# Converting float64 weights beside attention: the integer words in PSUM, the raw words in eleven buffers, and four stages a slot apart

## The chip, the cores and the metric

The kernel runs on one core of a Trainium2 chip. The core has TensorE (PE in the profile; its weight loads are PEld), VectorE (DVE), ScalarE (ACT), GpSimd (POOL) and SyncE (SP, which here only issues DMA transfers). SBUF is the on-chip memory of 128 partitions, PSUM the memory into which TensorE writes its products. The metric is the device time of one execution in microseconds (us). Each engine works through a queue of its own in a fixed order; a queue stands still while its next instruction waits for another engine or a transfer.

## The reference

Two steps follow each other. The first is attention over q, k and v of 4 batches, 8 heads, 768 positions, 64 dimensions, where a query sees the 8 first keys of its sequence and the 96 keys up to itself, with a bias by distance that has its own slope for each head:

```
scores = q @ k.T / 8 - slope[h] * dist      (-1e9 where not kept)
a = softmax(scores);  x = a @ v             x: [4, 768, 512]
```

The second is a channel mix over x, with weights w_k [512, 1024], w_v [1024, 512], w_r [512, 512] that come as float64:

```
xk = mu_k * x + (1 - mu_k) * x_prev         x_prev: the position before
xr = mu_r * x + (1 - mu_r) * x_prev
k = relu(xk @ w_k);  r = sigmoid(xr @ w_r)
out = r * ((k * k) @ w_v)
```

## The kernel before

**Tiles and chunks.** The 3072 positions are 24 tiles of 128 queries, and two tiles make a chunk of 256 positions for the channel mix, so there are 12 chunks. A loop over steps takes one tile at a time, in four slots (the loop variable hp, two heads each). In a slot stand the transposes of the tile before, the scores of this tile and pieces of channel mix of an earlier chunk; at a step's start stand the products with v of the tile two before.

**Attention of a tile.** Scores are products into PSUM; for the first seven tiles (NATIVE) they are plain float32 products (L287, with queries and keys in qz and kz), from tile 7 on they are products of float32r parts (L289, L290). VectorE adds the bias and takes the row's extreme (L295), ScalarE takes exp with the row sum (L296), VectorE makes the reciprocal r (L302, L303), GpSimd multiplies e by r (L306), TensorE transposes e (L317), ScalarE copies the transposes out of PSUM (et, L318), TensorE multiplies with v (av, L334), ScalarE copies the result to x (L345). Tiles 0, 6, 12 and 18 start a sequence and have 128 keys in place of 256.

**Channel mix.** Every factor is split in two float32r parts, hi and lo, and each product is hi·hi + lo·hi + hi·lo (L371, L372, L373). mix makes xk and xr: the part of x_prev on ScalarE for chunk 0 and on GpSimd for the others (L355, L357), the sum on VectorE (L358), hi on ScalarE (L359), lo on VectorE (L360). Products kp with w_k follow; each of the four results per chunk becomes kk (relu L397, square L398, hi L399, lo L400). Then come products z with w_r, the sigmoid, products vps with w_v, the last product on VectorE (L414), and the store. Chunk 0's channel mix is put in the queue at step 3, and slots then take up to five pieces each.

**Weights.** A float64 weight is made into hi + lo in blocks of 128 rows and 512 columns: 8 blocks of w_k, 4 of w_r, 8 of w_v, 20 in all (L140). A block comes by one transfer of 512 KB as pairs of 32-bit words (L159). ScalarE takes the absolute value of the upper words with a scale (L166, L169). A second scaling follows: on GpSimd for blocks 0 to 7 (L167), while blocks 8 to 19 are bounded on VectorE by a max and a min (L170). Three integer operations on VectorE build the float32 words: shift and mask (L171), sign (L172), bits of the lower word (L173). All of this is in place, in an SBUF tile a. Then hi is a copy in float32r on ScalarE (L174) or GpSimd (L196, pool_copy), two blocks each in turn, and lo = a - hi is a subtraction on GpSimd (L180).

**Where the raw words lie.** Blocks of w_r and w_v take a buffer of the pool p4k (tag t4k, three buffers), which serves the queries and keys of later tiles and the temporary of mix as well. Blocks of w_k take buffers of the channel mix (kk_hi, kk_lo, xk_hi, xk_lo, xr_hi, xr_lo) ahead of chunk 0. btmp, in which the bias patterns are made, has the buffer kk_hi.

**What sets the order.** The program is written for the Tile framework, which gives out a pool's buffers and lays down one order per engine by a planner with a cost model of its own. The source sets the sequence of requests: at the end of each slot (slot = 4 * step + hp) weights_go begins blocks up to a pace and ends those up to one fewer:

```
n = min(8, 2 + slot * 4 // 3) if slot < 6 else 8 + (slot - 5) * 6 // 7
weights_go(n, n - 1 if n <= len(w_steps) else n)
```

channel_mix also calls weights_need ahead of products, which forces what is not yet requested.

Of the kernel before, what the change touches and what calls it, by code (L numbers as in the profile page):

```python
# [33 lines left out]
def tile_biased_attention_channel_mix(ctx: ExitStack, tc: tile.TileContext, qT, kT, v, n_sizes, mu_kr, w_k, w_v, w_r, q_rows, k_rows, v_rows, slopes, out):  # L34
# [55 lines left out]
    # The distance; n_local for a key that is only global, which is over any distance of a local key;  # L90
    # FAR or more where masked: such a key's weight is exactly 0.
# [13 lines left out]
    # 96 keys before the tile, then the tile's own  # L105
# [9 lines left out]
    # tile 0  # L115
# [11 lines left out]
    # later tiles: 32 keys from the start, 96 keys before the tile, the tile  # L127
# [15 lines left out]

    def weight_begin(i):
        # A float64 weight's words: (sign, 11 exponent bits, 20 bits), (32 bits).
        # a: its first 24 significant bits as a float32; hi: a rounded to float32r; lo: the rest of a.
        name, src, k, c = w_steps[i]
        if name != "k":
            raw = p4k.tile([128, 512, 2], I32, tag="t4k", name=f"w64_{i}")
            a = f2_pool.tile([128, 512], I32, tag="f2", name=f"wa_{i}")  # L150
        elif k < 2:
            both = f_pool.tile([128, 2048], I32, tag=("kk_hi", "kk_lo")[k], name=f"w64_{i}")
            raw = both[:, 0:1024].rearrange("p (n w) -> p n w", w=2)
            a = both[:, 1024:1536]
        else:
            t = "xk" if k == 2 else "xr"
            raw = f_pool.tile([128, 512, 2], I32, tag=t + "_hi", name=f"w64_{i}")
            a = f_pool.tile([128, 512], I32, tag=t + "_lo", name=f"wa_{i}")
        nc.sync.dma_start(raw.rearrange("p n w -> p (n w)"), src[k * 128 : (k + 1) * 128, 2 * c : 2 * c + 1024])  # L159
        low, top = raw[:, :, 0], raw[:, :, 1]  # L160
        hi = wts[name][0][:, k, c : c + 512]
        # top's bits as a float32: times 2**-112 (or 2**16, which differs in a bit that the shift drops) moves the float64
        # exponent's bias to the float32's. What float32 cannot hold is bounded: from 2**128 up (by Inf, which stays Inf,
        # or the min) to a large number, under 2**-127 (by underflow or the max) to 0.
        if i < 8:
            act.activation(a.bitcast(F32), top.bitcast(F32), AF.Abs, scale=2.0**111)  # L166
            pool.tensor_scalar(a.bitcast(F32), a.bitcast(F32), 2.0**-112, 2.0**-111, op0=ALU.mult, op1=ALU.mult)  # L167
        else:
            act.activation(a.bitcast(F32), top.bitcast(F32), AF.Abs, scale=2.0**16)  # L169
            vec.tensor_scalar(a.bitcast(F32), a.bitcast(F32), 2.0, HUGE, op0=ALU.max, op1=ALU.min)  # L170
        vec.tensor_scalar(a, a, 3, 0x7FFFFFF8, op0=ALU.logical_shift_left, op1=ALU.bitwise_and)  # L171
        vec.scalar_tensor_tensor(a, top, -0x80000000, a, op0=ALU.bitwise_and, op1=ALU.bitwise_or)  # L172
        vec.scalar_tensor_tensor(a, low, 29, a, op0=ALU.logical_shift_right, op1=ALU.bitwise_or)  # L173
        (act.copy if i % 4 < 2 else pool_copy)(hi, a.bitcast(F32))  # L174
        w_live[i] = a
# [6 lines left out]
    w_count = [0, 0]  # L182

    def weights_go(begun, ended):
        while w_count[0] < min(begun, len(w_steps)):
            weight_begin(w_count[0])
            w_count[0] += 1
        while w_count[1] < min(ended, w_count[0]):
            weight_end(w_count[1])
            w_count[1] += 1  # L190
# [8 lines left out]
    state = {}  # L199
    # the first tiles' queries and keys, with 64 rows of zeros: products of all 128 rows keep the tensor engine's clock up  # L200
# [223 lines left out]
    LAG = 3  # tiles from a chunk's first to the start of its channel mix  # L424
# [214 lines left out]
```

## Time and profile before

| | |
|---|---|
| median of 3 runs | 526.06 us (525.92 to 526.25) |
| profiled execution: first to last instruction (span) | 524.1 us |
| what lies around the span, median less span | 1.96 us |
| PE busy | 495.9 us (95%) |
| DVE busy | 372.4 us (71%) |
| ACT busy | 323.6 us (62%) |
| POOL busy | 283.0 us (54%) |
| DMA | 48.16 MB, mean 92 GB/s |

The profiled execution's own time is taken as its span with those 1.96 us around it. A row of the page's groups or of an answer on groups reads: line, engine, operation, output<-input, shape, count | busy us, mean ns of one | idle time of the engine just before it, and what ended it. A row of waits reads: engine and line that waited <- engine and line that ended the wait: us in total, times, longest. A row of the timeline begins with its start and its length in us.

### The profile page before, as it was taken

The numbers are of one execution on the slowest core, as the hardware profiler recorded it, in microseconds if no ns is written. First come the engines' busy times: TensorE is split into PE (matmuls) and PEld (weight loads), VectorE is DVE, ScalarE is ACT, GpSimd is POOL, SyncE is SP. The second block draws the span as 40 slices with busy tenths as digits, with TensorE's granted clock in tenths as the row PEclk, the third lists the DMA queues.
The fourth block names the chain that finished last, engine by engine and source line by source line (L and its number), as shares of the span: only waits on it lengthen the run. The fifth ranks groups of instructions, "written<-read, shape, count | busy, mean of one in ns | idle before, by whom it ended". The sixth has DMA issues, their size and how long they took to land.

```text
span 524.1 us, 9900 instructions
## 1 busy us (share of the span) xinstructions
PE 495.9 (95%) x3466; PEld 427.2 (82%) x3466; DVE 372.4 (71%) x854; ACT 323.6 (62%) x730; POOL 283.0 (54%) x410
## 2 busy tenths in 40 slices
PE   7885888979999999999999999999999999999995
PEld 4563766869898898898898898898898898898984
DVE  6799999987677766767767867767777865535321
ACT  4868585823957856846847757756757667643220
POOL 8799977987355644544547645535547634203000
PEclk9979799999999999999999999999999999999999
DMA  8998268150350530530521431521422210000101
GB/s 197 322 232 198 67 185 188 41 144 20 107 134 6 141 107 5 157 91 8 162 76 38 130 86 34 133 86 59 124 62 66 62 46 26 35 12 2 41 1 44
DMA packets 27304, 48.16 MB, mean 92 GB/s; under 512 B 7216, under 2 KB 13360, under 8 KB 27248
## 3 DMA queue, kind: packets, MB, share of 16 engines
q1 hardware_dynamic: 27104, 47.46, 34.0%
q8 instruction: 29, 0.48, 0.4%
q14 instruction: 27, 0.22, 0.1%
q10 hardware_dynamic: 144, 0.00, 0.0%
HBM read 41.16 MB, written 6.29 MB: 91 GB/s over the span
## 4 chain that ended last, share of the span: by engine, by line
PE 80%; DVE 11%; POOL 5%; issue 3%; DMA 1%; ACT 0%; DVEq 0%; POOLq 0%
PE vps L372 8%; PE vps L373 8%; PE vps L371 8%; PE kp L371 8%; PE kp L373 8%; PE kp L372 8%; PE av L334 7%; PE t L317 6%; PE z L371 4%; PE z L373 4%; PE z L372 4%; PE s L290 3%; PE s L289 3%; POOL e L306 2%; PE s L287 2%
## 5 line engine op out<-in xcount | busy, mean ns | idle before, releaser
L306 POOL TENSOR_SCALAR e<-e,r 128x256 f32<-128x256 f32 (+1 forms) x192 | 106.1, 570 | 137.0 <-DVE r L303 91.9
L371 PE MATMUL kp<-xk_hi,wk_hi 128*128 128x256 f32 x384 | 108.0, 282 | 0.2 <-DVE kk L398 0.2
L373 PE MATMUL kp<-xk_hi,wk_lo 128*128 128x256 f32 x384 | 107.5, 280 | 0.5 <-POOL wk_lo L180 0.5
L372 PE MATMUL kp<-xk_lo,wk_hi 128*128 128x256 f32 x384 | 107.3, 279 | 0.0
L296 ACT ACTIVATE e<-e,nmax 128x256 f32<-128x256 f32 (+1 forms) x192 | 92.6, 484 | 22.0 <-DVE nmax L295 21.0
L295 DVE CUSTOM_DVE_ANT_0 e<-s,pat 128x256 f32<-128x256 f32 (+1 forms) x192 | 69.0, 395 | 31.0 <-PE s L290 21.2
L372 PE MATMUL vps<-wv_lo,kk_hi 128*128 128x512 f32 x192 | 76.0, 396 | 2.6 <-POOL wv_lo L180 2.6
L371 PE MATMUL vps<-wv_hi,kk_hi 128*128 128x512 f32 x192 | 75.9, 395 | 0.4 <-POOL wv_hi L196 0.4
L373 PE MATMUL vps<-wv_hi,kk_lo 128*128 128x512 f32 x192 | 75.8, 395 | 0.0
L371 PEld LDWEIGHTS kp<-xk_hi,wk_hi 128*128 128x128 f32 x384 | 72.9, 190 | 1.2 <-DVE kk L398 0.6
L373 PEld LDWEIGHTS kp<-xk_hi,wk_lo 128*128 128x128 f32 x384 | 72.8, 190 | 0.9 <-POOL wk_lo L180 0.9
L372 PEld LDWEIGHTS kp<-xk_lo,wk_hi 128*128 128x128 f32 x384 | 72.9, 190 | 0.6
L318 ACT COPY et<-t 128x512 f32<-128x512 f32 (+1 forms) x96 | 52.0, 546 | 20.2 <-PE t L317 19.7
L317 PE MATMUL t<-ident,e 128*128 128x128 f32 x352 | 57.5, 280 | 5.7 <-POOL e L306 5.6
L398 DVE TENSOR_TENSOR kk<-kp,kk 128x512 f32<-128x512 f32 x48 | 33.1, 689 | 41.2 <-ACT kk L397 41.0
L317 PEld LDWEIGHTS t<-ident,e 128*128 128x128 f32 x352 | 41.2, 141 | 19.1 <-POOL e L306 9.2
L334 PE MATMUL av<-et,va 128*64 128x128 f32 x704 | 49.4, 284 | 0.6 <-ACT et L318 0.6
L334 PEld LDWEIGHTS av<-et,va 128*64 128x64 f32 x704 | 40.3, 139 | 10.5 <-issue 5.8
L400 DVE TENSOR_TENSOR kk_lo<-kk,kk_hi 128x512 fp32r<-128x512 f32 x48 | 35.3, 735 | 17.4 <-ACT kk_hi L399 17.3
L399 ACT CAST kk_hi<-kk 128x512 fp32r<-128x512 f32 x48 | 29.8, 622 | 25.6 <-DVE kk L398 25.6
L397 ACT ACTIVATE kk<-kp 128x512 f32<-128x512 f32 x48 | 28.3, 590 | 26.7 <-PE kp L373 24.5
L372 PEld LDWEIGHTS vps<-wv_lo,kk_hi 128*128 128x128 f32 x192 | 36.0, 187 | 10.5 <-POOL wv_lo L180 3.1
(103 smaller groups left out, 1051.1 us busy)
## 6 DMA issues: line engine op xcount, KB each, us to landing
kraw<-in_kT_dram SPq DMA_DIRECT2D x36, 256.0 KB, 3.9
qraw<-in_qT_dram SPq DMA_DIRECT2D x34, 256.0 KB, 4.1
va<-in_v_dram SPq DMA_DIRECT2D x24, 256.0 KB, 3.1
out_dram<-sig SPq DMA_DIRECT2D x24, 256.0 KB, 3.5
w<-in_w_k_dram SPq DMA_DIRECT2D x8, 512.0 KB, 9.1
w<-in_w_v_dram SPq DMA_DIRECT2D x8, 512.0 KB, 3.5
kz<-in_kT_dram SPq DMA_DIRECT2D x8, 256.0 KB, 6.7
w<-in_w_r_dram SPq DMA_DIRECT2D x4, 512.0 KB, 9.3
```

The lines of the kernel that those rows point to most:

```text
L295: vec.tensor_tensor_reduce(out=e[:, :w], in0=o, in1=p[:, h, :], op0=ALU.add, op1=ALU.min, scale=-0.125, scalar=3.0e38, accum_out=s["nmax"] ...
L296: act.activation(e[:, :w], e[:, :w], AF.Exp, bias=s["nmax"][:, h : h + 1], scale=-1.0, accum_out=s["sum"][:, h : h + 1])
L306: pool.tensor_scalar(e[:, :w], e[:, :w], r[:, u : u + 1], 1.0, op0=ALU.mult, op1=ALU.mult)
L317: pe.transpose(pt[:, c : c + 128], e[:, k * 128 : (k + 1) * 128], ident)
L318: act.copy(et[:, : 2 * nb * 128], pt[:, : 2 * nb * 128])
L334: pe.matmul(o, vt[:, h * 64 : (h + 1) * 64], et[:, c : c + 128], start=k == 0, stop=k == nb - 1)
L371: pe.matmul(o, sh, mh, start=first, stop=False)
L372: pe.matmul(o, sh, ml, start=False, stop=False)
L373: pe.matmul(o, sl, mh, start=False, stop=last)
L398: vec.tensor_mul(kk, pv, kk)
L399: act.copy(kkh[:, 2 * fp : 2 * fp + 2, :], kk)
L400: vec.tensor_sub(kkl[:, 2 * fp : 2 * fp + 2, :], kk, kkh[:, 2 * fp : 2 * fp + 2, :])
```

## The change

The weights' work is cut into four functions, which the loop requests at the start of each slot, each at a pace of its own.

- weight_load only takes a buffer and issues the transfer. Raw words lie in eleven buffers: blocks 0 to 2 and 11 to 19 in t4k, blocks 3 to 6 in xk_hi, xr_hi, xk_lo, xr_lo, blocks 7 and 8 in the two halves of kk_lo, blocks 9 and 10 in those of kk_hi.
- weight_begin takes a tile a from the pool f2 for every block, has ScalarE take the absolute value (L163) and GpSimd do the second scaling (L164), now for all 20 blocks. The max and min on VectorE are gone.
- weight_bits does the three integer operations (L174, L175, L176). The words between them lie in bits, a PSUM tile of the pool ps_f, whose three banks kp, z and vps use; the third operation writes back to a. The copy to hi follows.
- weight_end is as before (L182).

With w_pace(slot), a slot requests ends up to w_pace(slot - 2), integer work up to w_pace(slot - 1), begins up to w_pace(slot) and loads up to w_pace(slot) + 5. Two loads are requested ahead of the loop. Comments were taken out as well, so that lines have other numbers after the change: scores L288, L290 and L291, e L296, r L303 and L304, normalise L307, transposes L318, av L335, mix L359 (sum) and L361 (lo), products L372 to L374, hi copies on GpSimd L197, transfers of weights L155, of queries and keys L224 to L232.

```diff
     w_live = {}
 
+    w_raw, w_two = {}, []
+
+    def weight_load(i):
+        name, src, k, c = w_steps[i]
+        if i < 3 or i > 10:
+            raw = p4k.tile([128, 512, 2], I32, tag="t4k", name=f"w64_{i}")
+        elif i < 7:
+            raw = f_pool.tile([128, 512, 2], I32, tag=("xk_hi", "xr_hi", "xk_lo", "xr_lo")[i - 3], name=f"w64_{i}")
+        else:
+            if i % 2:
+                w_two.append(f_pool.tile([128, 2, 512, 2], I32, tag=("kk_lo", "kk_hi")[i // 2 - 3], name=f"w64_{i}"))
+            raw = w_two[-1][:, (i - 7) % 2]
+        nc.sync.dma_start(raw.rearrange("p n w -> p (n w)"), src[k * 128 : (k + 1) * 128, 2 * c : 2 * c + 1024])
+        w_raw[i] = raw
+
     def weight_begin(i):
...
+        a = f2_pool.tile([128, 512], I32, tag="f2", name=f"wa_{i}")
+        act.activation(a.bitcast(F32), w_raw[i][:, :, 1].bitcast(F32), AF.Abs, scale=2.0**111)
+        pool.tensor_scalar(a.bitcast(F32), a.bitcast(F32), 2.0**-112, 2.0**-111, op0=ALU.mult, op1=ALU.mult)
+        w_live[i] = a
+
+    def weight_bits(i):
...
-        if i < 8:
-            act.activation(a.bitcast(F32), top.bitcast(F32), AF.Abs, scale=2.0**111)
-            pool.tensor_scalar(a.bitcast(F32), a.bitcast(F32), 2.0**-112, 2.0**-111, op0=ALU.mult, op1=ALU.mult)
-        else:
-            act.activation(a.bitcast(F32), top.bitcast(F32), AF.Abs, scale=2.0**16)
-            vec.tensor_scalar(a.bitcast(F32), a.bitcast(F32), 2.0, HUGE, op0=ALU.max, op1=ALU.min)
-        vec.tensor_scalar(a, a, 3, 0x7FFFFFF8, op0=ALU.logical_shift_left, op1=ALU.bitwise_and)
-        vec.scalar_tensor_tensor(a, top, -0x80000000, a, op0=ALU.bitwise_and, op1=ALU.bitwise_or)
-        vec.scalar_tensor_tensor(a, low, 29, a, op0=ALU.logical_shift_right, op1=ALU.bitwise_or)
+        bits = ps_f.tile([128, 512], I32, name=f"wb_{i}", tag="f")
+        vec.tensor_scalar(bits, a, 3, 0x7FFFFFF8, op0=ALU.logical_shift_left, op1=ALU.bitwise_and)
+        vec.scalar_tensor_tensor(bits, top, -0x80000000, bits, op0=ALU.bitwise_and, op1=ALU.bitwise_or)
+        vec.scalar_tensor_tensor(a, low, 29, bits, op0=ALU.logical_shift_right, op1=ALU.bitwise_or)
         (act.copy if i % 4 < 2 else pool_copy)(hi, a.bitcast(F32))
...
+    def w_pace(slot):
+
+        return max(0, min(8, slot * 4 // 3 + 1) if slot < 6 else 8 + (slot - 5) * 5 // 4)
+
     load_tile(0)
     split_tile(0)
+    weights_go(0, 2)
...
         for hp in range(4):
+            slot = 4 * step + hp
+            weights_go(3, w_pace(slot - 2))
+            weights_go(2, w_pace(slot - 1))
+            weights_go(1, w_pace(slot))
+            weights_go(0, w_pace(slot) + 5)
...
-            slot = 4 * step + hp
-            n = min(8, 2 + slot * 4 // 3) if slot < 6 else 8 + (slot - 5) * 6 // 7
-            weights_go(n, n - 1 if n <= len(w_steps) else n)
```

The planner lays down another order for the first seven tiles. TensorE is shown first, where channel mix starts: s, t, av are scores, transposes and products with v; the number at a name's end is a tile's allocation. Before, the first kp stands among the transposes of tile 4, right behind the scores s_2 of that tile:

```order
96 L287 MATMUL s_2_890<-kz_178,qz_177 128x256 x2
97 L334 MATMUL av_729<-et_3_676,va_305 64x128
98 L334 MATMUL av_729<-et_3_676,va_413 64x128
99 L334 MATMUL av_729<-et_3_676,va_305 64x128
100 L334 MATMUL av_729<-et_3_676,va_413 64x128
101 L317 MATMUL t_0_750<-ident,e_0_582 128x128 x2
102 L371 MATMUL kp<-xk_hi,wk_hi 128x256 x2
103 L317 MATMUL t_0_750<-ident,e_1_585 128x128 x2
```

Now it stands behind the last scores of tile 6 (s_3_1441) and six of that tile's eight transposes:

```order
159 L288 MATMUL s_3_1441<-kz_178,qz_177 128x128 x2
160 L318 MATMUL t_1_1311<-ident,e_3_1118 128x128 x2
...
168 L318 MATMUL t_1_1561<-ident,e_3_1324 128x128
169 L318 MATMUL t_2_1610<-ident,e_4_1389 128x128
170 L318 MATMUL t_2_1610<-ident,e_5_1392 128x128
171 L372 MATMUL kp<-xk_hi,wk_hi 128x256 x2
172 L373 MATMUL kp<-xk_lo,wk_hi 128x256
173 L374 MATMUL kp<-xk_hi,wk_lo 128x256
```

What moved is chunk 0's channel mix, from tile 4's scores to behind tile 6's. Rows 171 to 467 now hold 192 kp, 42 z and 48 vps products and the products of tile 5 with v; at row 468 come tile 7's first scores. That row was row 467 before, and from there on both orders read alike.

On VectorE the place is the mix of chunk 0 (mix_k, and xk_lo which the first kp's last part needs). Before, it stands among blocks 5 to 7 and the scores of tiles 3 and 4:

```order
120 L171 TENSOR_SCALAR wa_322<-wa_322 128x512
121 L172 SCALAR_TENSOR_TENSOR wa_322<-w_6_321,wa_322 128x512
122 L358 SCALAR_TENSOR_TENSOR mix_k<-x_424,mus,mix_k 128x256
...
127 L358 SCALAR_TENSOR_TENSOR mix_k<-x_424,mus,mix_k 128x256
128 L173 SCALAR_TENSOR_TENSOR wa_322<-w_6_321,wa_322 128x512
129 L171 TENSOR_SCALAR w_5_291<-w_5_291 128x512
130 L358 SCALAR_TENSOR_TENSOR mix_k<-x_424,mus,mix_k 128x256 x2
```

Now it stands behind block 17 and among block 18, when the scores of all seven tiles have been taken:

```order
215 L304 RECIPROCAL r_3_1450<-r_3_1450 128x4
216 L174 TENSOR_SCALAR wb_707<-wa_673 128x512
217 L175 SCALAR_TENSOR_TENSOR wb_707<-w_17_494,wb_707 128x512
218 L176 SCALAR_TENSOR_TENSOR wa_673<-w_17_494,wb_707 128x512
219 L359 SCALAR_TENSOR_TENSOR mix_k<-x_461,mus,mix_k 128x256
220 L174 TENSOR_SCALAR wb_733<-wa_712 128x512
221 L359 SCALAR_TENSOR_TENSOR mix_k<-x_461,mus,mix_k 128x256 x2
```

The mix moved from block 6's integer work to that of blocks 17 and 18. The third place is SP's queue of transfers ahead of tile 2's queries and keys. Before:

```order
7 L239 DMA va_192<-in_v_dram 128x512
8 L159 DMA w_1_211<-in_w_k_dram 128x1024
9 L159 DMA w_2_238<-in_w_k_dram 128x1024
10 L159 DMA w_3_257<-in_w_k_dram 128x1024
11 L230 DMA kz_178<-in_kT_dram 64x8x32
12 L223 DMA qz_177<-in_qT_dram 64x1024
```

Now, with two weight blocks ahead of tile 1's data as well (rows 4 and 5):

```order
10 L155 DMA w_2_201<-in_w_k_dram 128x1024
11 L155 DMA w_3_203<-in_w_k_dram 128x1024
12 L155 DMA w_4_205<-in_w_k_dram 128x1024
13 L155 DMA w_5_207<-in_w_k_dram 128x1024
14 L155 DMA w_6_226<-in_w_k_dram 128x1024
15 L155 DMA w_7_255<-in_w_k_dram 128x1024
16 L155 DMA w_7_255<-in_w_r_dram 128x1024
17 L155 DMA w_9_279<-in_w_r_dram 128x1024
18 L224 DMA qz_177<-in_qT_dram 64x1024
```

Tile 2's queries moved from behind three weight blocks to behind ten.

More of the change, by code (lines that the diff above doesn't have):

```diff
@@ L29 @@
 FAR = 1.0e12
-HUGE = (1.875 - 2.0**-13) * 2.0**32
 @with_exitstack
@@ L142, in tile_biased_attention_channel_mix @@
     w_live = {}
-    def weight_begin(i):
-        name, src, k, c = w_steps[i]
[L148 to L154, printed above, removed]
-        else:
[L156 to L159, printed above, removed]
+    w_raw, w_two = {}, []
@@ L160, in weight_begin @@
+    def weight_begin(i):
+        a = f2_pool.tile([128, 512], I32, tag="f2", name=f"wa_{i}")
[3 more added lines that the diff above has]
+    def weight_bits(i):
+        name, src, k, c = w_steps[i]
+        a, raw = w_live[i], w_raw.pop(i)
         low, top = raw[:, :, 0], raw[:, :, 1]
         hi = wts[name][0][:, k, c : c + 512]
-        if i < 8:
-            act.activation(a.bitcast(F32), top.bitcast(F32), AF.Abs, scale=2.0**111)
-            pool.tensor_scalar(a.bitcast(F32), a.bitcast(F32), 2.0**-112, 2.0**-111, op0=ALU.mult, op1=ALU.mult)
-        else:
-            act.activation(a.bitcast(F32), top.bitcast(F32), AF.Abs, scale=2.0**16)
-            vec.tensor_scalar(a.bitcast(F32), a.bitcast(F32), 2.0, HUGE, op0=ALU.max, op1=ALU.min)
@@ L174, in weight_begin @@
+        vec.scalar_tensor_tensor(a, low, 29, bits, op0=ALU.logical_shift_right, op1=ALU.bitwise_or)
         (act.copy if i % 4 < 2 else pool_copy)(hi, a.bitcast(F32))
-        w_live[i] = a
     def weight_end(i):
@@ L180, in weight_end, with weights_go @@
         pool.tensor_sub(lo, w_live.pop(i).bitcast(F32), hi)
[L182 to L190, printed above, removed]
+    w_stages = (weight_load, weight_begin, weight_bits, weight_end)
+    w_count = [0, 0, 0, 0]
+    def weights_go(stage, n):
+        while w_count[stage] < min(n, len(w_steps)):
+            w_count[stage] += 1
+            w_stages[stage](w_count[stage] - 1)
     def weights_need(n):
-        weights_go(n, n)
+        for stage in range(4):
+            weights_go(stage, n)
     def pool_copy(dst, src):
```

## The prediction

> **What bounds the kernel now.** I read the page's busy times first, then windows by stage, then what TensorE waited for in the first 120 us, then the groups of VectorE and GpSimd there. In the windows the columns are PE, PEld, DVE, ACT and POOL busy time with counts, then the granted TensorE clock, the DMA share and GB/s.
>
> ```profile
> PE 495.9 (95%) x3466; PEld 427.2 (82%) x3466; DVE 372.4 (71%) x854; ACT 323.6 (62%) x730; POOL 283.0 (54%) x410
> ```
>
> ```profile
> 0.00:40.00 40.00, 32.13 (x150) 21.16 (x150) 32.23 (x116) 26.27 (x79) 34.45 (x52) 0.91 1.05 251
> 40.00:80.00 40.00, 30.91 (x212) 24.81 (x212) 38.69 (x89) 29.42 (x78) 34.77 (x40) 0.91 0.54 144
> 80.00:120.00 40.00, 34.40 (x229) 28.45 (x228) 37.24 (x70) 21.35 (x47) 33.06 (x35) 1.00 0.49 127
> 120.00:400.00 280.00, 280.00 (x2070) 249.07 (x2071) 205.59 (x457) 187.50 (x414) 148.85 (x227) 1.00 0.30 82
> 400.00:524.10 124.10, 118.49 (x814) 103.72 (x810) 58.62 (x126) 59.10 (x114) 31.93 (x59) 0.99 0.11 35
> ```
>
> From 120 to 400 us TensorE is busy without a gap. Of its 28.2 us of idle time (524.1 - 495.9), 22.6 lie before 120 us (7.9 + 9.1 + 5.6) and 5.6 in the tail. The page would call the kernel TensorE's, but a change to the weights can move only the first 120 us, and there VectorE and GpSimd are the full engines: between 40 and 80 us VectorE works 38.7 of 40 us. What TensorE waited for says the same:
>
> ```profile
> PE s L287 <- DVE nmax L295: 6.8, 3, 3.2
> PE t L317 <- POOL e L306: 5.6, 10, 1.2
> PE vps L372 <- POOL wv_lo L180: 2.6, 2, 1.8
> ```
>
> So the useful question is at which time TensorE reaches the stretch that it alone bounds, and how much of its work it has then done.
>
> **The mark.** The two TensorE orders shown with the change meet at the first score product of tile 7. Behind that row they read alike, and before it both hold the same products. Before, TensorE gets there at 131.63:
>
> ```profile
> 54.79 0.48 PE L371 MATMUL kp<-xk_hi,wk_hi 128*128 128x256 f32 x2
> 58.31 0.42 PE L371 MATMUL kp<-xk_hi,wk_hi 128*128 128x256 f32 x1
> 58.52 0.41 PE L372 MATMUL kp<-xk_lo,wk_hi 128*128 128x256 f32 x1
> 62.24 0.28 PE L372 MATMUL kp<-xk_lo,wk_hi 128*128 128x256 f32 x1
> 62.95 0.28 PE L372 MATMUL kp<-xk_lo,wk_hi 128*128 128x256 f32 x1
> 131.63 0.37 PE L289 MATMUL s<-kw,qh 128*128 128x256 f32 x1
> 133.60 0.39 PE L371 MATMUL vps<-wv_hi,kk_hi 128*128 128x512 f32 x1
> 135.46 0.39 PE L373 MATMUL vps<-wv_hi,kk_lo 128*128 128x512 f32 x1
> ```
>
> The difference of two starts, over the steps between them, is an instruction's pitch: kp (62.95 - 62.24) / 6 = 0.118, vps (135.46 - 133.60) / 8 = 0.2325 us, and z has vps's shape. The first kp comes at 54.8 us, so channel-mix products fill TensorE while the other engines still convert blocks 9 to 19 and work through tiles 4 to 6. In the changed order no channel-mix product stands ahead of row 171, which is behind all seven native tiles' scores and the transposes of tile 6's e_5. From row 171 to the mark come 192 kp, 42 z, 48 vps and 16 av products, with nothing of the attention's scores between: 192 x 0.118 = 22.7, 42 x 0.2325 = 9.8, 48 x 0.2325 = 11.2, 16 av about 1.0, in sum 44.7 us. If T0 is the time of the first kp, the mark moves to T0 + 44.7, plus what the stretch loses. I count 2 us for a low clock at its start: the first kp products, at 58.31 and 58.52, stand 0.21 apart, and only some 4 us later they go at 0.118, so about half of that time is lost; the first kp there too came after TensorE had waited. I add 1 us for stalls at a new chunk's kk_lo on VectorE, between 0 and 3. **Break-even is thus T0 = 131.6 - 47.7 = 83.9 us.**
>
> **Cost of the parts on VectorE.** Window 14 to 110 us, by form:
>
> ```profile
> L295 DVE CUSTOM_DVE_ANT_0 e<-s,pat 128x256 f32<-128x256 f32 x40 | 15.2, 414 | 3.6 <-PE s L287 2.3 <-PE t L317 1.3
> L173 DVE SCALAR_TENSOR_TENSOR wa<-w,wa 128x512 int32<-128x512 int32 x16 | 15.1, 948 | 0.0
> L172 DVE SCALAR_TENSOR_TENSOR wa<-w,wa 128x512 int32<-128x512 int32 x16 | 12.6, 795 | 0.1
> L170 DVE TENSOR_SCALAR wa<-wa 128x512 f32<-128x512 f32 x12 | 10.4, 874 | 0.0
> L171 DVE TENSOR_SCALAR wa<-wa 128x512 int32<-128x512 int32 x16 | 8.5, 535 | 0.0
> L171 DVE TENSOR_SCALAR w<-w 128x512 int32<-128x512 int32 x4 | 3.3, 820 | 1.0 <-POOL w L167 1.0
> L173 DVE SCALAR_TENSOR_TENSOR w<-w 128x512 int32<-128x512 int32 x4 | 2.9, 734 | 0.0
> L172 DVE SCALAR_TENSOR_TENSOR w<-w 128x512 int32<-128x512 int32 x4 | 2.7, 682 | 0.0
> L398 DVE TENSOR_TENSOR kk<-kp,kk 128x512 f32<-128x512 f32 x4 | 2.7, 676 | 0.0
> ```
>
> The weights take 15.1 + 12.6 + 10.4 + 8.5 + 3.3 + 2.9 + 2.7 = 55.5 us of VectorE. The 12 clips go: -10.4. An integer operation with a PSUM operand isn't in the trace; the nearest row is L398, 512 elements with one operand in PSUM, at 676 ns. Bounds: 535 ns (the cheapest of the three kinds now) and 950 ns (the dearest). I take 676: 60 x 0.676 = 40.6 us, so VectorE is relieved by about 15 us (at the bounds 23 and -1.5).
>
> The Trainium skill ("VectorE: DVE Perf Modes", "Why PSUM operands drop a tier") says that a PSUM operand holds an fp32 operation to the basic rate. It speaks against L171's move; by 676 in place of its 535 ns the 20 blocks would lose 2.8 us there, and no run here yet shows it.
>
> **Cost of the parts on GpSimd.** The scaling of blocks 8 to 19 moves here: 12 more L167, 0.656 to 0.846 each, +8 to +10 us. Window 14 to 110 us, then the two normalise groups between 200 and 400 us:
>
> ```profile
> L306 POOL TENSOR_SCALAR e<-e,r 128x256 f32<-128x256 f32 x40 | 32.0, 814 | 8.4 <-DVE r L303 8.4
> L180 POOL TENSOR_TENSOR wv_lo<-wa,wv_hi 128x512 fp32r<-128x512 f32 x7 | 11.0, 1576 | 0.2
> L180 POOL TENSOR_TENSOR wk_lo<-wa,wk_hi 128x512 fp32r<-128x512 f32 x4 | 5.3, 1343 | 0.1
> L306 POOL TENSOR_SCALAR e<-e,r 128x128 f32<-128x128 f32 x9 | 4.9, 557 | 0.4 <-DVE r L303 0.4
> L167 POOL TENSOR_SCALAR wa<-wa 128x512 f32<-128x512 f32 x4 | 3.4, 846 | 0.9 <-ACT wa L166 0.9
> L167 POOL TENSOR_SCALAR w<-w 128x512 f32<-128x512 f32 x4 | 2.6, 656 | 0.0
> L196 POOL TENSOR_SCALAR wk_hi<-wa 128x512 fp32r<-128x512 f32 x4 | 2.8, 711 | 0.0
> ```
>
> ```profile
> L306 POOL TENSOR_SCALAR e<-e,r 128x256 f32<-128x256 f32 x64 | 30.8, 498 | 58.9 <-DVE r L303 43.1 <-ACT et L318 13.6 <-ACT x L345 2.2
> L306 POOL TENSOR_SCALAR e<-e,r 128x128 f32<-128x128 f32 x16 | 5.7, 372 | 12.2 <-ACT kk L397 9.3 <-DVE r L303 2.9
> ```
>
> The same normalise takes 814 ns while VectorE is full and 498 where it is not: GpSimd is slowed by what VectorE does beside it. Its own queue decides T0, since the transposes ahead of row 171 need the e's of tile 6. In the changed order GpSimd has, from its first normalise (12.63 us before) to that one, 40 + 14 normalises, 19 scalings, 17 low parts, 8 hi copies and the kw copies of tiles 7 and 8 (about 3.4 us; the first is 1.91 in the row below). At the quiet ends of these rows: 40 x 0.498 + 14 x 0.372 + 19 x 0.656 + 17 x 1.343 + 8 x 0.70 + 3.4 = 69.7. At the crowded ends: 40 x 0.814 + 14 x 0.557 + 19 x 0.846 + 17 x 1.576 + 8 x 0.711 + 3.4 = 92.3. With a third of VectorE's weight time gone I stand a little above the quiet end, at 73 us: the normalises at 570, the page's mean for the whole span, the rest as in the quiet sum.
>
> ```profile
> L306 POOL TENSOR_SCALAR e<-e,r 128x256 f32<-128x256 f32 (+1 forms) x192 | 106.1, 570 | 137.0 <-DVE r L303 91.9
> 12.63 1.07 POOL L306 TENSOR_SCALAR e<-e,r 128x128 f32<-128x128 f32 x3 [1.09 <-DVE nmax L295]
> 116.67 1.91 POOL L196 TENSOR_SCALAR kw<-kraw 128x2048 fp32r<-128x2048 f32 x1 [2.14 <-PE s L287]
> sum 97.37, PE 79.61 PEld 61.21 DVE 92.28 ACT 67.42 POOL 84.62; mean PE 15.92 PEld 12.24 DVE 18.46 ACT 13.48 POOL 16.92
> ```
>
> From 12.63 to 110 us GpSimd idles 97.37 - 84.62 = 12.75 us now, mostly for r from VectorE. I keep 5 of it, as VectorE gets slack. **T0 = 12.6 + 73 + 5 = about 90.6; say 90 us.**
>
> The Trainium skill ("SBUF — State Buffer", "SBUF: two separate sides") calls the port that VectorE and GpSimd share an exclusive lock, which VectorE takes in its two-port modes or with two SBUF inputs. The rows 814 against 498 agree that the two disturb each other. With the words in PSUM none of the three operations has two SBUF inputs, so by this rule GpSimd would run at the quiet ends; that result is the first rival.
>
> **Other edits.** ScalarE keeps its 20 Abs and its copies, and TensorE its products: nothing. The words' tiles take banks from the three that kp, z and vps use; only block 19's is still live when the first kp starts, so no product waits there, and nothing is added. Loads: in SP's changed order, shown with the change, tile 2's queries and keys stand behind ten weight blocks. Seven of these were not ahead of them before: 7 x 0.512 MB at 291 GB/s (next row) is 12 us by which tile 2 comes later. VectorE and GpSimd fill that time with blocks 0 to 5, so it costs nothing as long as the queue of GpSimd, not the tiles' data, sets T0; else up to 5 us, inside the idle time above.
>
> ```profile
> 12.63:30.00 17.37, 14.20 (x83) 9.16 (x81) 13.98 (x51) 14.97 (x47) 14.25 (x22) 1.00 1.13 291
> ```
>
> Why chunk 0's mix comes so late: its buffer is one of the three t4k, which now hold raw blocks up to 17 and 18 first. So the order puts mix_k on VectorE behind block 17's integer work. The mix itself costs what it did; what is late next is the whole first channel mix.
>
> **Sum.** Mark at 90 + 44.7 + 2 + 1 = 137.7, 6.1 us later than 131.6. Behind it nothing differs, so the span becomes 530.2. The shown times have a median of 526.06, 1.96 above the span; with that around it, **532 us, 1.2% slower**.
>
> **Rivals.** First, faster: GpSimd at its quiet ends with 2 us of idle time gives T0 = 12.6 + 66 to 70 + 2, about 82, and less where a low part falls under its 1.34; the mark comes at 129 and the time is about 524. For it: L306's 498 with VectorE at 73% busy (205.59 of 280). Against it: 12 scalings more, and 69.7 is already the sum with every group at its best row. It decides from T0 under 83. Second, no change: T0 between 83 and 85, the channel mix lost in front and the relief cancel; 526. Third, much slower: the crowded ends persist because the integer work itself is what disturbs GpSimd, wherever its words lie, and the three raw buffers for blocks 11 to 19 pass through load, Abs, scaling and three operations one after another: T0 = 12.6 + 85 + 3, about 101, mark 149, time 543. Against it: 15 us less on VectorE. Fourth, that the late start costs nothing since TensorE had no use for the time: then all 22.6 us of idle would have to stay as they are, but in the new order only the attention of seven tiles stands ahead of T0, so idle time before T0 must grow unless T0 is early; I give it nothing beside the first.
>
> **Chances.** My forecast (T0 86 to 96, time 528 to 538) 0.5; much slower 0.18; no change 0.11; faster 0.21. One can tell 0.2% from no change here, about 1 us. The range from 522 to 543 leaves out some 0.1 at each end; the forecast's own is 528 to 538. Faster 0.21, within 0.2% 0.11, slower 0.68.
>
> **What would show it.** First kp near 90 us and 44 to 48 us of unbroken products to tile 7's first score near 138; L307's mean 500 to 620 ns before T0; L174 to L176 0.6 to 0.7 us each; TensorE's idle before 120 us some 6 us up. I am wrong if the first kp comes before 84 us, if products stall after it by more than 4 us, or if stretches behind the mark differ.

## The result and the profile after

The changed kernel takes 547.2 us (median of 4, 545.2 to 551.1), the kernel before 526.2 us (4 runs, 525.9 to 526.9): a ratio of 1.041, 95% interval 1.037 to 1.045. It is slower by 21 us where 6 were forecast; the range ended at 543.

The page's busy times of the changed kernel, profiled at a span of 549.3 us:

```profile
PE 502.2 (91%) x3466; PEld 432.8 (79%) x3466; DVE 357.2 (65%) x842; ACT 322.1 (59%) x728; POOL 265.3 (48%) x422
```

VectorE, ScalarE and GpSimd all work less than before (372.4, 323.6 and 283.0), and the kernel is slower. Next stand windows that end at 120 us, at tile 7's first scores (the mark) and at the end, of the changed kernel and then of the kernel before; the columns are those of the prediction.

```profile
0.00:120.00 120.00, 78.47 (x438) 58.54 (x439) 83.91 (x247) 67.57 (x190) 87.33 (x140) 0.82 0.71 160
120.00:157.20 37.20, 37.20 (x238) 32.07 (x236) 18.29 (x24) 13.26 (x21) 3.89 (x5) 1.00 0.16 43
157.20:549.30 392.10, 386.49 (x2794) 342.21 (x2792) 255.00 (x572) 241.25 (x517) 174.04 (x278) 1.00 0.25 70
```

```profile
0.00:120.00 120.00, 97.44 (x589) 74.42 (x590) 108.16 (x273) 77.03 (x202) 102.27 (x125) 0.94 0.69 174
120.00:131.60 11.60, 11.60 (x82) 10.28 (x82) 9.15 (x9) 3.43 (x6) 7.85 (x7) 1.00 0.05 14
131.60:524.10 392.50, 386.89 (x2798) 342.51 (x2796) 255.06 (x573) 243.17 (x523) 172.93 (x278) 1.00 0.25 69
```

Behind the mark both take 392 us with the same work. The whole loss, 25.2 us between these two executions, lies ahead of it: the mark moved from 131.6 to 157.2. In the first 120 us TensorE is busy 19 us less, and at a granted clock of 0.82 instead of 0.94.

TensorE's timeline of the changed kernel, at the first kp and at the mark:

```profile
108.00 0.58 PE L372 MATMUL kp<-xk_hi,wk_hi 128*128 128x256 f32 x1 [4.96 <-ACT xk_hi L360]
157.25 0.38 PE L290 MATMUL s<-kw,qh 128*128 128x256 f32 x1
```

From the first kp to the mark it takes 49.2 us, against 47.7 in the forecast. What failed is T0: 108 instead of 90 us. The groups of VectorE from 12 to 120 us (all 20 blocks), those of GpSimd from 12 to 110 us, and the sum of windows from 12 to 110 us show that the durations were not the reason:

```profile
L174 DVE TENSOR_SCALAR wb<-wa 128x512 int32<-128x512 int32 x20 | 13.7, 686 | 1.5 <-POOL wa L164 1.5
L175 DVE SCALAR_TENSOR_TENSOR wb<-w,wb 128x512 int32<-128x512 int32 x20 | 13.7, 686 | 0.1
L176 DVE SCALAR_TENSOR_TENSOR wa<-w,wb 128x512 int32<-128x512 int32 x20 | 13.6, 680 | 0.1
```

```profile
L307 POOL TENSOR_SCALAR e<-e,r 128x256 f32<-128x256 f32 x40 | 18.5, 480 | 2.3 <-DVE r L304 2.3
L164 POOL TENSOR_SCALAR wa<-wa 128x512 f32<-128x512 f32 x20 | 12.4, 620 | 5.6 <-ACT wa L163 5.5
L182 POOL TENSOR_TENSOR wk_lo<-wa,wk_hi 128x512 fp32r<-128x512 f32 x8 | 10.1, 1287 | 1.3 <-ACT wk_hi L177 1.1
```

```profile
sum 98.00, PE 59.91 PEld 43.64 DVE 67.33 ACT 59.46 POOL 68.70; mean PE 11.98 PEld 8.73 DVE 13.47 ACT 11.89 POOL 13.74
```

The three integer operations cost 41.0 us in all (forecast 40.6). A normalise fell from 814 to 480 ns and a scaling to 620, so GpSimd works 68.7 us between 12 and 110 us: the quiet sum of the prediction, 69.7, and not the 73 taken. But GpSimd idles 29.3 of these 98 us and VectorE 30.7. In the forecast GpSimd idled 5.

The Trainium skill ("SBUF — State Buffer", "SBUF: two separate sides") names a VectorE operation in a two-port mode or with two SBUF inputs as what locks out GpSimd. The row 814 to 480 agrees, and so does 487 in b_psum below, where the words in PSUM are the only edit. Which of the two conditions counted, no run separates.

What the engines wait for, TensorE in the first 200 us and then VectorE from 12 to 110 us:

```profile
PE t L318 <- POOL e L307: 12.1, 4, 7.1
PE s L288 <- DMA kz<-in_kT_dram: 11.6, 4, 4.3
PE kp L372 <- ACT xk_hi L360: 5.0, 1, 5.0
```

```profile
DVE e L296 <- PE s L288: 14.7, 7, 4.2
DVE e L296 <- PE t L318: 6.9, 4, 3.1
DVE r L303 <- ACT e L297: 6.2, 6, 1.8
```

TensorE waits 11.6 us for keys (2.2 before), and VectorE 14.7 us for the scores of them. TensorE's timeline has the place: first scores of tiles 2 and 3, before and then in the changed kernel.

```profile
19.96 1.53 PE L287 MATMUL s<-kz,qz 128*128 128x256 f32 x6 [0.95 <-DMA kz<-in_kT_dram]
34.09 3.74 PE L287 MATMUL s<-kz,qz 128*128 128x256 f32 x8
```

```profile
36.07 3.75 PE L288 MATMUL s<-kz,qz 128*128 128x256 f32 x8 [1.91 <-DMA kz<-in_kT_dram]
49.44 3.75 PE L288 MATMUL s<-kz,qz 128*128 128x256 f32 x8 [3.88 <-DMA kz<-in_kT_dram]
```

Both tiles come 15 to 16 us later. At the other end stands the chain that releases the first kp (timeline of the changed kernel, rows of DVE, SP, ACT, POOL and PE):

```profile
85.81 0.69 DVE L176 SCALAR_TENSOR_TENSOR wa<-w,wb 128x512 int32<-128x512 int32 x1
86.82 0.34 SPq L240 DMA_DIRECT2D va<-in_v_dram  x1
87.27 1.69 SPq L155 DMA_DIRECT2D w<-in_w_v_dram  x1
91.93 0.68 ACT L163 ACTIVATE wa<-w 128x512 f32<-128x512 f32 x1 [1.08 <-DMA w<-in_w_v_dram]
94.37 3.84 DVE L303 TENSOR_SCALAR r<-sum 128x4 f32<-128x4 f32 x1 [1.83 <-ACT e L297]
94.51 0.62 POOL L164 TENSOR_SCALAR wa<-wa 128x512 f32<-128x512 f32 x1
95.10 2.50 POOL L182 TENSOR_TENSOR wv_lo<-wa,wv_hi 128x512 fp32r<-128x512 f32 x2
97.55 0.64 POOL L164 TENSOR_SCALAR wa<-wa 128x512 f32<-128x512 f32 x1
98.24 2.29 DVE L267 TENSOR_TENSOR kw<-kraw,kw 64x2048 fp32r<-64x2048 f32 x1
100.66 0.67 DVE L174 TENSOR_SCALAR wb<-wa 128x512 int32<-128x512 int32 x1
102.09 0.69 DVE L176 SCALAR_TENSOR_TENSOR wa<-w,wb 128x512 int32<-128x512 int32 x1
102.22 0.82 PE L318 MATMUL t<-ident,e 128*128 128x128 f32 x2 [7.14 <-POOL e L307]
102.81 1.71 ACT L356 ACTIVATE mix_k<-x,mus 128x256 f32<-128x256 f32 x4 [4.91 <-DVE wa L176]
106.90 1.04 ACT L360 CAST xk_hi<-mix_k 128x1024 fp32r<-128x1024 f32 x1 [1.87 <-DVE mix_k L359]
```

Chunk 0's mix on ScalarE waits 4.9 us for block 17's third integer operation (L176, at 102.09), whose raw t4k buffer it takes. That block's words came late: its load goes out at 87.27, behind a v transfer at 86.82 for which SP waited 4.1 us, and 0.8 us after block 14's third operation (85.81 to 86.50) gave back the t4k buffer that it takes; the words land at 91.93. VectorE stood still over L303 besides, and tile 6's last transposes, behind which kp stands, waited 7.1 us for normalises. TensorE is busy 1.9 us of the last 14 ahead of 108. This bears out the wait for t4k that the prediction named, but not its date.

### The profile page after: what moved, and what is told of

Read it like the earlier page. It is cut to its first block, busy times and chain, and to the rows that moved or that the text cites. A ratio compares the mean times of both kernels' runs of the same rounds, so it can differ in the third digit from the quotient of the medians.

```text
span 549.3 us, 9899 instructions
## 1 busy us (share of the span) xinstructions
PE 502.2 (91%) x3466; PEld 432.8 (79%) x3466; DVE 357.2 (65%) x842; ACT 322.1 (59%) x728; POOL 265.3 (48%) x422
## 5 line engine op out<-in xcount | busy, mean ns | idle before, releaser
L307 POOL TENSOR_SCALAR e<-e,r 128x256 f32<-128x256 f32 (+1 forms) x192 | 88.6, 479 | 132.7 <-DVE r L304 81.5
L372 PE MATMUL kp<-xk_hi,wk_hi 128*128 128x256 f32 x384 | 108.0, 282 | 5.0 <-ACT xk_hi L360 5.0
L374 PE MATMUL kp<-xk_hi,wk_lo 128*128 128x256 f32 x384 | 107.4, 280 | 0.0
L296 DVE CUSTOM_DVE_ANT_0 e<-s,pat 128x256 f32<-128x256 f32 (+1 forms) x192 | 69.0, 397 | 54.3 <-PE s L291 26.9
L372 PEld LDWEIGHTS kp<-xk_hi,wk_hi 128*128 128x128 f32 x384 | 73.1, 191 | 5.8 <-ACT xk_hi L360 5.2
L374 PE MATMUL vps<-wv_hi,kk_lo 128*128 128x512 f32 x192 | 75.9, 395 | 0.0
L372 PE MATMUL vps<-wv_hi,kk_hi 128*128 128x512 f32 x192 | 75.8, 395 | 0.0
L374 PEld LDWEIGHTS kp<-xk_hi,wk_lo 128*128 128x128 f32 x384 | 72.9, 190 | 0.0
L318 PE MATMUL t<-ident,e 128*128 128x128 f32 x352 | 58.5, 291 | 15.5 <-POOL e L307 12.1
L318 PEld LDWEIGHTS t<-ident,e 128*128 128x128 f32 x352 | 43.2, 147 | 28.0 <-POOL e L307 18.4
L335 PE MATMUL av<-et,va 128*64 128x128 f32 x704 | 49.9, 284 | 6.0 <-ACT e L297 2.4
L335 PEld LDWEIGHTS av<-et,va 128*64 128x64 f32 x704 | 40.3, 139 | 16.3 <-ACT e L297 6.7
L401 DVE TENSOR_TENSOR kk_lo<-kk,kk_hi 128x512 fp32r<-128x512 f32 x48 | 34.0, 707 | 19.4 <-ACT kk_hi L400 19.4
L288 PE MATMUL s<-kz,qz 128*128 128x256 f32 (+1 forms) x112 | 34.3, 456 | 13.3 <-DMA kz<-in_kT_dram 11.6
```

The costliest lines, as they stand in the source:

```text
L288: pe.matmul(o, s["qr"][:, h, :], s["kr"][:, h, c0:256], start=True, stop=True)
L296: vec.tensor_tensor_reduce(out=e[:, :w], in0=o, in1=p[:, h, :], op0=ALU.add, op1=ALU.min, scale=-0.125, scalar=3.0e38, accum_out=s["nmax"] ...
L307: pool.tensor_scalar(e[:, :w], e[:, :w], r[:, u : u + 1], 1.0, op0=ALU.mult, op1=ALU.mult)
L318: pe.transpose(pt[:, c : c + 128], e[:, k * 128 : (k + 1) * 128], ident)
L335: pe.matmul(o, vt[:, h * 64 : (h + 1) * 64], et[:, c : c + 128], start=k == 0, stop=k == nb - 1)
L372: pe.matmul(o, sh, mh, start=first, stop=False)
```

## Experiments

A gate is here a buffer whose release holds back the work that takes it next. Theory A: chunk 0's channel mix is held back by buffers, the t4k buffers that its mix shares with raw words, and the three PSUM banks that kp shares with integer words. Theory B: weight blocks requested too early put their transfers in front of the tiles' data, and everything comes late. All ratios are against the kernel before; a plain difference between two runs' times is a difference of medians.

**Words in SBUF again, in the changed kernel, and words in PSUM alone, in the kernel before.**

```diff
-        bits = ps_f.tile([128, 512], I32, name=f"wb_{i}", tag="f")
-        vec.tensor_scalar(bits, a, 3, 0x7FFFFFF8, ...)
+        vec.tensor_scalar(a, a, 3, 0x7FFFFFF8, ...)
...
```

> The changed kernel with one edit: the integer words in place in SBUF. The order of TensorE keeps the first kp at row 171. Theory of my forecast (GpSimd's and VectorE's busy time sets the first kp): L307 goes back to 0.75 to 0.85 us from 0.48, GpSimd works 15 to 20 us more, time 555 to 565. Theory B (waits for transfers and buffers set it): the engines have 29 to 31 us of idle time to take it in, time 545 to 552.

552.5 us, ratio 1.051 (1.049 to 1.054). Its group of normalises and its largest wait of TensorE:

```profile
L306 POOL TENSOR_SCALAR e<-e,r 128x256 f32<-128x256 f32 x40 | 26.8, 687 | 0.0
```

```profile
PE t L317 <- POOL e L306: 18.5, 15, 4.1
```

The contention is back in part (687 ns instead of 480; before the change it was 814). GpSimd works 85.7 us between 12 and 110 us, 17 more than in the changed kernel, as the forecast's theory had it, and yet this costs only 5 us: most of it fits into time in which the engines wait anyway. The time lies 0.5 us above theory B's range, and below the forecast's.

> The kernel before with one edit: the integer words between the three operations in PSUM tiles of ps_f. The planner then puts the first kp behind tile 6's scores (row 190, before: 102), and tile 7's first scores at row 386. Theory A (PSUM banks as a gate): slower, 530 to 540, in spite of normalises at 0.5 us. If relief of GpSimd and VectorE outweighs it: 515 to 523.

535.4 us, ratio 1.017 (1.014 to 1.019): slower alone, though its normalises take 487 ns. The same edit for the eight blocks of w_k only (words stay in PSUM for i < 8, in a otherwise):

> The kernel before with words in PSUM for the eight blocks of w_k alone. First kp at row 115 (before: 102), and tile 7's first scores at row 472. Relief without a gate: VectorE and GpSimd save together some 6 to 10 us ahead of 115 us, time 518 to 524. If the planner's other order takes it back: 526 to 532.

526.1 us (10 runs), ratio 0.999 (0.998 to 1.000): no change.

```profile
L361 DVE TENSOR_TENSOR xk_lo<-mix_k,xk_hi x12: 1210/1214/1261, 79.6 to 494.9; 128x1024 fp32r<-128x1024 f32 x12
```

```profile
93.52 0.56 PE L372 MATMUL kp<-xk_hi,wk_hi 128*128 128x256 f32 x1
```

```profile
L375 PE MATMUL kp<-xk_hi,wk_hi x384: 276/276/775, 62.1 to 501.5; 128*128 128x256 f32 x192
```

With all words in PSUM (the first two rows), xk_lo is finished by 81 us, and kp still starts at 93.5, since its place in the order is behind tile 6's last transposes (the last start at 93.18). With the late blocks' words in SBUF (the third row) it starts at 62. So PSUM words of blocks 8 to 19 cost about 9 us, as far as the traces show through the order that they bring about. That the three shared banks make the planner do so is argued from the source, in which these blocks ask for banks ahead of kp; no run gave the words banks of their own.

**The scaling alone, and the eleven buffers alone, in the kernel before.** The first replaces `if i < 8` by `if i < 20` in weight_begin. The second takes the change's buffers and its tile a, and keeps words in SBUF, max and min on VectorE, and the old pace.

> The kernel before with one edit: the second scaling of blocks 8 to 19 on GpSimd in place of the max and min on VectorE. First kp at row 115 (before: 102). VectorE loses 10 us of work and GpSimd gets 8 to 10. If GpSimd's queue is what is late in the first 120 us: 529 to 535. If VectorE's is: 518 to 524. If they trade evenly: 525 to 528.

532.2 us, ratio 1.012 (1.010 to 1.013). Its normalises, and its window of the first 120 us:

```profile
L306 POOL TENSOR_SCALAR e<-e,r 128x256 f32<-128x256 f32 x40 | 35.2, 896 | 1.8 <-DVE r L303 1.8
```

```profile
0.00:120.00 120.00, 98.13 (x565) 71.77 (x566) 96.39 (x256) 75.41 (x202) 111.09 (x138) 0.90 0.69 169
```

They went from 814 to 896 ns, and GpSimd works 111 us of the first 120, where it was 102: its queue was late, as the first of the three expectations had it.

> The raw buffers alone: eleven buffers as in the change, every a in f2, but words in SBUF, max and min on VectorE for blocks 8 to 19, and the pace of the kernel before. First kp at row 81 (before: 102), six blocks ahead of tile 2. a_bpacesbuf differs only by the scaling on GpSimd, which alone cost 6 us in b_pool. If costs add: 522 to 526. If the blocks ahead of tile 2 cost what the earlier kp brings: 526 to 531.

534.3 us, ratio 1.015 (1.014 to 1.017), a miss: the first kp starts at 50.2 us, 4.6 earlier than before, and the kernel is 8 us slower. Costs of the parts don't add: with the scaling on GpSimd as well (a_bpacesbuf below) it is 530.1. A part of the loss is in the trace: six blocks stand ahead of tile 2, whose first scores come at 27.1 us instead of 20.0, and between 20 and 40 us VectorE works 15.4 us instead of 19.0. Tile 2 comes as late in a_bpacesbuf, so this is not what makes the two differ; that stays open, and the planner's order differs in both.

**The t4k gate.** In the changed kernel, chunk 0's mix temporary in kk_hi and kk_lo, which are free by then:

```diff
-        tmp = tmp_pool.tile([128, 4, 256], F32, name=f"mix_{tag}", tag="t4k")
+        if on_act:
+            tmp = f_pool.tile([128, 4, 256], F32, name=f"mix_{tag}", tag="kk_hi" if tag == "k" else "kk_lo")
+        else:
+            tmp = tmp_pool.tile([128, 4, 256], F32, name=f"mix_{tag}", tag="t4k")
```

> The changed kernel with one edit: the temporary of chunk 0's mix lies in kk_hi and kk_lo, not in t4k; integer words stay in PSUM. Theory A with t4k as the gate: the mix is done by 80 us, time 530 to 536. Theory A with the three PSUM banks as the second gate (kp asks for a bank behind the words of blocks up to 14 or later): first kp after 95 us still, but fewer products in front of tile 7's first scores, time 538 to 546. Theory B: 545 to 549.

540.5 us, ratio 1.028 (1.022 to 1.033): 7 us back, with the first kp at 99.6 still, though ScalarE now starts the mix at 61.2 us instead of 102.8. As expected for t4k with a second gate behind it.

> The changed kernel with two edits: the three integer operations in place in SBUF again, and the temporary of chunk 0's mix in kk_hi and kk_lo instead of a t4k buffer. On TensorE the first kp then stands among tile 5's transposes again (row 120 in place of 171). Theory A (the loss is that chunk 0's channel mix is held back, by t4k buffers and by PSUM banks): first kp 30 to 45 us earlier than 108, time 526 to 533. Theory B (the loss is the ten weight blocks ahead of tile 2's data and the long way through load, Abs, scaling and three operations): both stay, time 540 to 548.

543.2 us, ratio 1.032 (1.030 to 1.034). First kp at 79.7, 28 us earlier than 108, and only 4 us of time gained (9 against a_sbuf, which has the same words in SBUF). Theory A alone falls here, by its time of 526 to 533: an early first kp is worth little by itself. That what follows it in the queue isn't ready is the likely reason, and is not shown.

**Fewer blocks ahead of tile 2.** Three as before, and the change's pace from slot 4 on:

```diff
-            weights_go(0, w_pace(slot) + 5)
+            weights_go(0, w_pace(slot) + 5 if slot > 3 else 3)
```

(moved ahead of the other stages, none of which runs ahead of the loads).

> The changed kernel, but only three weight blocks are requested ahead of tile 2's queries and keys, and no stage runs ahead of the loads; from slot 4 on the pace is the change's. TensorE's first kp stays behind tile 6's scores (row 172). Theory B (the ten blocks ahead of tile 2 make attention late, 36 us in place of 20 for tile 2's first scores): tile 2 back near 20 us, first kp 12 to 16 us earlier than 108, time 531 to 537. Theory A (t4k and PSUM gates alone): first kp within 5 us of 108, time 542 to 549.

541.5 us, ratio 1.028 (1.026 to 1.030). The time lies between the two theories' ranges, and the first kp comes at 98.0, 10 us earlier. Tile 2's scores come at 22 us again, but the wait has only moved to the next tile (its first scores were at 34.09 before):

```profile
44.66 4.82 PE L288 MATMUL s<-kz,qz 128*128 128x256 f32 x12 [3.34 <-DMA kz<-in_kT_dram]
```

With both edits, and then with words in PSUM only for blocks 0 to 10 as well:

> Both edits: three blocks ahead of tile 2, and chunk 0's mix temporary outside t4k. If the two losses add (a_mix gave 7 of 21 us back): 524 to 531. If each only uncovers the other gate, the three PSUM banks: 535 to 541.

537.3 us, ratio 1.018 (1.015 to 1.022).

> As a_mixcap, and integer words lie in PSUM only for blocks 0 to 10, in place in SBUF for 11 to 19, so kp's banks don't wait for the late blocks; first kp at row 128, before tile 6's scores. If PSUM banks are the last gate: first kp by 75 us, time 518 to 526. If contention of the late blocks or their long way takes it back: 528 to 536.

539.8 us, ratio 1.028 (1.023 to 1.032), above both ranges, with the first kp at 74.2: taking the late words out of PSUM brings kp 25 us forward and no time. It also brings contention back (normalises at 644 ns, 512 in a_mixcap), so the bank's share is not read cleanly from it. The first loads and the t4k gate together were worth 10 us, and 11 us remained: the pace from slot 4 on, or the scaling.

**The pace.** At the end of each slot, all stages by the number of the kernel before, in the changed kernel (the two loads ahead of the loop go too):

```diff
-            weights_go(3, w_pace(slot - 2))
-            weights_go(2, w_pace(slot - 1))
-            weights_go(1, w_pace(slot))
-            weights_go(0, w_pace(slot) + 5)
...
+            n = min(8, 2 + slot * 4 // 3) if slot < 6 else 8 + (slot - 5) * 6 // 7
+            weights_go(0, n)
+            weights_go(1, n)
+            weights_go(2, n)
+            weights_go(3, n - 1 if n <= len(w_steps) else n)
```

> The changed kernel with the pace of the kernel before: at the end of a slot load, begin, integer work up to the same number, ends up to one fewer. Eleven buffers, words in PSUM, and scaling on GpSimd stay. Six blocks stand ahead of tile 2 (change: ten, before: three); first kp at row 158, tile 7's first scores at row 382. If the pace is the main loss (a_cap, which slowed only the first loads, gave 6 us back): 527 to 535. If the gates are: 540 to 546.

529.3 us (10 runs, 525.8 to 532.5), ratio 1.007 (1.004 to 1.009): 18 of the 21 us are the pace. It opens the t4k gate as well: ScalarE starts chunk 0's mix at 35.5 us.

> As a_bpace, and chunk 0's mix temporary outside t4k; first kp at row 147, and tile 7's first scores behind the whole channel mix at row 475 again. Gates by t4k and pace were the loss: 523 to 531. PSUM banks hold kp back still: 533 to 540.

527.1 us, ratio 1.002 (0.999 to 1.005).

> As a_bpace, with the integer words in place in SBUF: what is left of the change is eleven buffers and the scaling on GpSimd. First kp at row 81 (before: 102). If no gate is left and the order decides: 522 to 530, with normalises near 0.8 us again. If GpSimd's 12 more scalings decide: 530 to 538.

530.1 us, ratio 1.008 (1.006 to 1.009). With the old pace, words in PSUM or in SBUF make no difference that shows (1.007 against 1.008). The time lies on the border of the two expected ranges and decides for neither.

The pace is three things. One load ahead of the begins instead of five (`w_pace(slot) + 1`, requested ahead of the other stages):

> The changed kernel with one number changed: loads are requested one block ahead of begins, not five. Rate (5/4 of a block a slot) and stages a slot apart stay. Six blocks stand ahead of tile 2, as in a_bpace; first kp at row 188. If the loads' lead is what the pace costs (a_bpace gave 18 of 21 us back): 529 to 535. If rate or stages cost it: 539 to 546.

535.6 us, ratio 1.020 (1.017 to 1.024): 11.6 us back. The window of the first 120 us, and TensorE's first scores of tile 2:

```profile
0.00:120.00 120.00, 85.80 (x536) 67.40 (x537) 101.60 (x261) 75.45 (x203) 93.05 (x144) 0.84 0.70 174
```

```profile
26.74 3.52 PE L288 MATMUL s<-kz,qz 128*128 128x256 f32 x8 [2.17 <-DVE wa L176]
```

TensorE is busy 7.3 us more in these 120 us than in the changed kernel, and VectorE 17.7: it has the scores earlier and goes on with them. Tile 2 doesn't wait for its keys any more, and all waits for keys fall from 11.6 to 4.6 us. But this edit works through theory A as well: with fewer loads asked for ahead of it, chunk 0's mix gets its t4k buffer earlier, and ScalarE starts it at 74.6 us instead of 102.8. The 11.6 us are thus both theories together, about what a_mixcap got back with one edit for each (10 us; a_cap and a_mix alone 6 and 7). How they divide here, no run separates.

> The changed kernel with begin, integer work and end of a block in one slot (end one block behind), as fast as the begins of the change a slot later; loads five ahead as in the change. Ten blocks ahead of tile 2. If the slots between the stages cost the time: 529 to 536. If the loads' lead does: 541 to 549.

Ratio 1.034 (1.029 to 1.038), which is 544 us: the slots between the stages are worth about 4 us, by the intervals 1 to 7, and the lead of the loads stays the main cost.

With the lead of one, and the rate back to `8 + (slot - 5) * 6 // 7`:

> As a_lead, and the rate after slot 6 back to 6/7 of a block a slot; stages stay a slot apart. First kp at row 139 (a_lead: 188). a_lead left 10 us over the kernel before, a_bpace 3. If the rate is that difference (all 20 blocks asked for before kp asks for its bank): 528 to 532. If the slots between the stages are: 534 to 538.

530.5 us, ratio 1.009 (1.005 to 1.013): another 5 us. Window and first kp:

```profile
0.00:120.00 120.00, 95.91 (x579) 74.59 (x580) 102.55 (x263) 75.60 (x204) 99.23 (x148) 0.87 0.72 174
```

```profile
L372 PE MATMUL kp<-xk_hi,wk_hi x384: 276/276/513, 70.9 to 503.6; 128*128 128x256 f32 x192
```

The first kp comes at 70.9 us, where it was at 98.3 with the lead alone. There xk_hi was ready at 82.3 us, and kp stood behind transposes that waited 13.4 us in all for normalises; now these waits are 0.5 us. That the late blocks' words ask for their PSUM banks behind kp at the slower rate, and so leave it its earlier place, is argued from the source. TensorE is 95.9 us busy, almost what it was before the change (97.4). Stages still a slot apart cost nothing here that can be told from a_bpace's 1.007.

**Towards something better than both.**

> As a_bpacemix (before's pace, mix temporary outside t4k, words in PSUM), but three blocks ahead of tile 2 as in the kernel before. If tile 2's late data still costs some 5 us there (8.5 us of TensorE waiting for kz in a_bpacemix): 520 to 524. If VectorE and GpSimd only fill that wait with the blocks' work: 525 to 529.

527.5 us, ratio 1.002 (1.001 to 1.003). Its waits for kz are still there, and the engines fill them:

```profile
PE s L288 <- DMA kz<-in_kT_dram: 6.7, 3, 3.7
```

> As b_hyb8 (before with PSUM words for the blocks of w_k), and blocks 9, 12, 15, 18 scaled on GpSimd. VectorE was full there from 30 to 90 us and GpSimd at 80 to 90%. If VectorE's 4 x 0.87 us less come through: 521 to 525. If GpSimd, crowded again by the words in SBUF, is as full: 526 to 530.

528.3 us, ratio 1.004 (1.003 to 1.006): VectorE's relief by four clips was spent on GpSimd again. No version was faster than the kernel before.

The chain from the changed kernel back, by ratios:

| edit, each added to the one above | ratio | 95% interval |
|---|---|---|
| the change | 1.041 | 1.037 to 1.045 |
| loads one block ahead, not five | 1.020 | 1.017 to 1.024 |
| 6/7 of a block a slot, not 5/4 | 1.009 | 1.005 to 1.013 |
| stages and loads in one slot, at its end | 1.007 | 1.004 to 1.009 |
| chunk 0's mix temporary outside t4k | 1.002 | 0.999 to 1.005 |

The intervals of the first three rows are clear of each other; each of the last two overlaps the one above it.

## Why the prediction was wrong

- **What bounds, and the mark.** Right. All of the change lies ahead of tile 7's first scores (392.1 and 392.5 us behind them), and the stretch from first kp to there takes 49.2 us, 47.7 by the sum.
- **VectorE's durations.** Right: 0.684 us for an integer operation with PSUM, 0.676 taken. The first of the three agrees with the Trainium skill ("VectorE: DVE Perf Modes", "Why PSUM operands drop a tier"): 686 ns where it took 535 in place in 16 of the 20 blocks. The other two got faster (795 to 686, 948 to 680 in these blocks); that they had been slowed by GpSimd beside them is likely and not shown.
- **GpSimd's durations.** Too careful: 73 us were taken between two sums, and the quiet one was measured (68.7; its terms add up to 69.4, not 69.7, and nothing hangs on that). The first rival had this half right. Its other half, 2 us of idle time, is what made its time, 524, and was as wrong as the forecast's 5.
- **Idle time ahead of T0: the step that failed.** "I keep 5 of it, as VectorE gets slack" became 29.3 us. The forecast took GpSimd's queue as the thing that sets T0 and gave the rest as cover. The sentence on the loads is where it went wrong: seven more blocks ahead of tile 2's data "costs nothing", or "up to 5 us, inside the idle time above". Tile 2 and tile 3 came 15 to 16 us later, and the work that was to fill the time was too short: VectorE waited 14.7 us for scores. Loads asked for five blocks ahead in place of one are worth 11.6 us (547.2 against 535.6), through late keys and the t4k gate together, and the faster rate another 5.
- **The gate.** The mix behind block 17 was seen, but priced by GpSimd's queue alone. Its date comes from that block's load, which SP issues at 87.3 us, behind a v transfer that waited for TensorE and 0.8 us after block 14 gave its buffer back. Moving the mix's temporary gave 7 us in the changed kernel and 2 with the old pace.
- **PSUM banks "nothing is added".** Not so in the order: words of blocks 8 to 19 in PSUM took the kernel before from 526.1 to 535.4 us. In the changed kernel, taking out those of blocks 11 to 19 (a_mixcap to a_mixcaphyb) gave nothing.
- **The third rival** had a similar time (543) from two reasons. One, contention that persists, was wrong (480 ns). The other, three raw buffers through which blocks 11 to 19 pass one after another, shows in the changed kernel: the loads of blocks 18 and 19 wait 1.4 and 1.3 us for the third operations that free their buffers, and block 17's goes out right behind one. Its nearness in time is half luck.
- **Still open.** How the lead's 11.6 us divide between late keys and the t4k gate; why the eleven buffers alone cost 8 us, beyond tile 2's 7 us of delay; whether a PSUM bank of their own would let the words keep their gain.

## What to carry to other kernels

A queue's busy time bounds a stretch from below, and a sum of durations should then be held against what each engine waits for in the new order: here work fell on three engines and the kernel lost 21 us, 18 of them through the pace: transfers were requested early and fast, on the queue that also loads the attention's tiles and into buffers that chunk 0's mix takes as well. Before a transfer is moved ahead, list what stands behind it on its queue and behind it in its buffer pool, and who has nothing else to do until that comes. And a scratch tile put into a shared pool, in SBUF or in PSUM, also moves the work that takes the next buffer: look for that work's new place in each engine's order before counting the gain.

## What the runs showed of the hardware that was not expected

VectorE can be held by GpSimd for a long time. In the chain above, L303 works on 128 x 4 elements (172 ns in the median of this trace) and takes 3.84 us, from 94.37 to 98.21, while GpSimd goes without a gap through a scaling, two low parts and a scaling from 94.51 to 98.19. The trace of a_lead has it again: an L303 of 4.66 us ends at 38.73, and GpSimd works without a gap up to 38.70. The Trainium skill ("SBUF — State Buffer", "SBUF: two separate sides") has the lock held for a whole instruction; here VectorE got no turn between four of them.

The 10 runs of a_bpace spread over 7 us (525.8 to 532.5), where the kernel before stays within 525.5 and 527.0 in 16. The cause is not shown: a_bpacemixcap, in which TensorE waits 6.7 us for keys as well, stays within 1.7 us in 11 runs.
